# A new schedule for a decayed linear attention with a maxout layer behind it: items of 256 tokens, 64x64 tensor tiles, and an order planned at build time

## The chip, the cores and the metric

The kernel runs on one core of one Trainium2 chip. The metric is device time in microseconds, from the start of the program to its end; lower is better. The engines of the core work side by side and are named here as the profile names them: PE is TensorE (matrix multiply), PEld its loading of weights, DVE is VectorE, ACT is ScalarE, POOL is GpSimd, SP is SyncE, which here only issues transfers. A transfer (DMA) moves data between the chip's main memory and the core's on-chip memory; matrix products land in PSUM, which has eight banks.

## The reference

Inputs are q, k, v and alpha of 4 sequences, 8 heads, 768 tokens and 48 features, and three weight matrices. A state of 48 x 48 for each head decays by alpha and takes in k times v at every token; its product with q is the attention output. The heads are then joined to 384 features per token (3072 tokens in all), and a maxout layer follows.

```python
for t in range(S):
    state = alpha[:, :, t, :, None] * state + np.einsum('bhd,bhe->bhde', k[:, :, t], v[:, :, t])
    y[:, :, t] = np.einsum('bhd,bhde->bhe', q[:, :, t], state)
...
x = attn_out.transpose(0, 2, 1, 3).reshape(B * S, H * D)     # 3072 x 384
h1 = x @ w1                                                  # w1, w2: 384 x 1024
h2 = x @ w2
out = np.maximum(h1, h2) @ w_out                             # w_out: 1024 x 384
```

Everything is given and returned in float32.

## The kernel before

The recurrence is computed in chunks of 128 tokens, 24 of them ("items"). The logarithm of alpha is summed along the chunk by a matmul (`cs`); its exponentials scale q and k (`qt`, `kt`), both are turned by PE, scores are `kt` times `qt` under a triangular mask (`pt`), and `y` is the masked scores times v plus q times the carried state (`T16`). The state itself goes on through `kv` and `w`.

```python
def load(n):                        # four transfers of 192 KB, rows of 48 floats (192 bytes)
    b, c = divmod(n, NCH)
    for src, tag in ((alpha, "af"), (q, "qf"), (k, "kf"), (v, "vf")):
        t = ldp.tile([128, H, D], FP32, tag=tag, name=tag)
        nc.sync.dma_start(out=t, in_=src[b, :, c * C : (c + 1) * C, :].rearrange("h p d -> p h d"))
...
def p1(n):                          # PE: sums of the logarithm
    nc.tensor.matmul(cs[:, 0 : H * D], lhsT=cmat, rhs=loga[:, :, 0:D], start=True, stop=True)
    for r in range(NP):             # four small ones, whole-chunk sums
        nc.tensor.matmul(cs[0:112, o : o + 2], lhsT=lp[:, r, 0:112], rhs=gcol, start=True, stop=True)
def a2(n):                          # ACT: en, ep, gg (exponentials, written to SBUF)
    nc.scalar.activation(out=en, in_=csv, func=ACTF.Exp, scale=-1.0)
    nc.scalar.activation(out=ep, in_=csv, func=ACTF.Exp)
...
def v1(n):                          # qt on DVE, kt on POOL, v to 16 bit on POOL
    nc.vector.tensor_mul(out=qts[n % 2][:, :, 0:D], in0=qf, in1=s["ep"])
    nc.gpsimd.tensor_mul(out=kts[n % 2][:, :, 0:D], in0=kf, in1=s["en"])
...
def p2(n):                          # PE: eight transposes of 128 columns; v2 copies them to SBUF (qk)
    for r in range(NP):
        nc.tensor.transpose(tp[:, r, :], qp[:, r, :], ident16)
    for r in range(NP):
        nc.tensor.transpose(tp[:, NP + r, :], kp[:, r, :], ident16)
...
def p3(n):                          # PE: scores (two row tiles) and kv (two column tiles)
    for r in range(NP):
        for o, ps in ((0, pa), (64, pb)):
            nc.tensor.matmul(ps[:, r, :], lhsT=qk[o : o + D, NP + r, :], rhs=qk[o : o + D, r, :], ...)
...
def p4(n):                          # PE: y in blocks of 32 features, four column tiles
    for i in range(3):
        if not first:
            for r in range(NP):
                nc.tensor.matmul(y[32 * r : 32 * r + 32, i, :], lhsT=T16[0:112, r, i, :], rhs=s["qk"][0:112, r, :], ...)
        for t in range(2):
            for r in range(NP):
                nc.tensor.matmul(y[32 * r : 32 * r + 32, i, :], lhsT=v16[:, r, i, 16 * t : 16 * t + 32],
                                 rhs=s["pt"][:, t, r, :], ...)
```

The maxout layer uses max(h1, h2) = h2 + relu(h1 - h2). So only `h` = x (w1 - w2) goes through relu, and the part with h2 is x times m, where m = w2 w_out is computed once on the chip (`prep_t`, `prep_m`). `h` is made for groups of mostly 384 tokens, `op` for each 128.

```python
def fstep(a, W, f):                 # h for one of 8 blocks of 128 features, W tokens; relu on ACT or DVE
    for s in range(3):
        nc.tensor.matmul(h[:, 0:W], lhsT=wd16[:, s, f * 128 : (f + 1) * 128], rhs=xT[:, s, a : a + W], ...)
def tstep(a, i, half):              # out for 128 tokens: 3 matmuls with m, 8 with w_out; ACT evicts, SP stores
    ...
```

The order is written by hand: in each round the loads five items ahead, parts of three items' attention, and in between the gaps are filled from a list of dense steps (`gap`).

```python
for n in range(1, NCG + 1):
    if n - 1 + LD < NCG:
        load(n - 1 + LD)
    v1(n + 1)
    if n > 1:
        p4(n - 1)
        a3(n - 1)
    gap(1.05)
    ...
```

PSUM is split into three pools of three, two and three banks. Item 0 is loaded first, then w2, w1 and w_out as one transfer each, then items 1 to 4.

Of the kernel before, what the change touches and what calls it, by code (L numbers as in the profile page):

```python
# [9 lines left out]
FP16 = mybir.dt.float16  # L10
FP32 = mybir.dt.float32
ACTF = mybir.ActivationFunctionType
ALU = mybir.AluOpType


@with_exitstack
def kernel(
# [15 lines left out]

    nc = tc.nc
    B, H, S, D = q.shape
    C = 128
    NCH = S // C
    NCG = B * NCH  # L40
    NP = H // 2
    NT, DM = out.shape
    DFF = moe_w1.shape[1]
    NF = DFF // 128
    WMAX = 384

    ctx.enter_context(tc.manual_schedule())
    constp = ctx.enter_context(tc.tile_pool(name="constp", bufs=1))
    ldp = ctx.enter_context(tc.tile_pool(name="ldp", bufs=6))
    wk = ctx.enter_context(tc.tile_pool(name="wk", bufs=2))  # L50
    mo = ctx.enter_context(tc.tile_pool(name="mo", bufs=2))
    psx = ctx.enter_context(tc.tile_pool(name="psx", bufs=3, space=bass.MemoryType.PSUM))
    psp = ctx.enter_context(tc.tile_pool(name="psp", bufs=2, space=bass.MemoryType.PSUM))
    psm = ctx.enter_context(tc.tile_pool(name="psm", bufs=3, space=bass.MemoryType.PSUM))

    LD = 5
    nc.scalar.preload_act_table_set("natural_log_exp_and_others")

    loads = {}

    def load(n):
        b, c = divmod(n, NCH)
        got = []
        for src, tag in ((alpha, "af"), (q, "qf"), (k, "kf"), (v, "vf")):
            t = ldp.tile([128, H, D], FP32, tag=tag, name=tag)
            nc.sync.dma_start(  # L66
                out=t, in_=src[b, :, c * C : (c + 1) * C, :].rearrange("h p d -> p h d")
            )
            got.append(t)
        loads[n] = got  # L70


    w1f = constp.tile([128, 3, DFF], FP32)
    w2f = constp.tile([128, 3, DFF], FP32)
    wof = constp.tile([128, NF, DM], FP32)
# [6 lines left out]
    load(0)  # L82
    nc.sync.dma_start(out=w2f, in_=moe_w2.rearrange("(p s) f -> p s f", s=3))
    nc.sync.dma_start(out=w1f, in_=moe_w1.rearrange("(p s) f -> p s f", s=3))
    nc.sync.dma_start(out=wof, in_=moe_w_out.rearrange("(s p) d -> p s d", p=128))
    for n in range(1, LD):
        load(n)

    ident16 = constp.tile([128, 128], FP16)
    make_identity(nc, ident16)  # L90
    u16 = constp.tile([128, 128], FP16)
    make_upper_triangular(nc, u16, val=1.0, diag=True)
    half1 = constp.tile([128, 128], FP16)
    nc.gpsimd.memset(half1, 0.0)
    nc.gpsimd.memset(half1[0:64, :], 1.0)
    cmat = constp.tile([128, 128], FP16)
    nc.vector.tensor_sub(out=cmat, in0=u16, in1=half1)
    gcol = constp.tile([128, 2], FP16)
    nc.gpsimd.memset(gcol, 0.0)
    nc.gpsimd.memset(gcol[0:64, 0:1], 1.0)  # L100
    nc.gpsimd.memset(gcol[64:128, 1:2], 1.0)

    NB = 3
    logas = [constp.tile([128, H, 64], FP16, name=f"loga{i}") for i in range(2)]
    qts = [constp.tile([128, H, 64], FP16, name=f"qt{i}") for i in range(2)]
    kts = [constp.tile([128, H, 64], FP16, name=f"kt{i}") for i in range(2)]

    v16s = [constp.tile([128, NP, 3, 48], FP16, name=f"v16_{i}") for i in range(NB)]
    T16s = [constp.tile([128, NP, 3, 32], FP16, name=f"T16_{i}") for i in range(NB)]
    for i in range(2):  # L110
        for t in (logas, qts, kts):
            nc.vector.memset(t[i], 0.0)
    for t in v16s + T16s:
        nc.gpsimd.memset(t, 0.0)

    xT = constp.tile([128, 3, NT], FP16)


    st = {}

    def a1(n):
        if n < NCG:
            nc.scalar.activation(out=logas[n % 2][:, :, 0:D], in_=loads[n][0], func=ACTF.Ln)  # L123

    def p1(n):
        if n >= NCG:
            return
        loga = logas[n % 2]
        cs = psx.tile([128, H * D + 2 * NP], FP32, tag="x", name="cs")
        nc.tensor.matmul(cs[:, 0 : H * D], lhsT=cmat, rhs=loga[:, :, 0:D], start=True, stop=True)  # L130
        lp = loga.rearrange("p (r t) d -> p r (t d)", t=2)
        for r in range(NP):
            o = H * D + 2 * r
            nc.tensor.matmul(cs[0:112, o : o + 2], lhsT=lp[:, r, 0:112], rhs=gcol, start=True, stop=True)  # L134
        st[n] = {"cs": cs}

    def a2(n):
        if n >= NCG:
            return
        cs = st[n]["cs"]  # L140
        csv = cs[:, 0 : H * D].rearrange("p (h d) -> p h d", h=H)
        ep = wk.tile([128, H, D], FP32, tag="ep")
        en = wk.tile([128, H, D], FP32, tag="en")
        gg = wk.tile([128, NP, 2], FP32, tag="gg", bufs=4)
        nc.scalar.activation(out=en, in_=csv, func=ACTF.Exp, scale=-1.0)  # L145
        nc.scalar.activation(out=ep, in_=csv, func=ACTF.Exp)  # L146
        nc.scalar.activation(
            out=gg[0:112], in_=cs[0:112, H * D :].rearrange("p (r t) -> p r t", t=2), func=ACTF.Exp
        )
        st[n].update(ep=ep, en=en, gg=gg)  # L150

    def v1(n):
        if n >= NCG:
            return
        _, qf, kf, vf = loads[n]
        s = st[n]
        nc.vector.tensor_mul(out=qts[n % 2][:, :, 0:D], in0=qf, in1=s["ep"])  # L157
        nc.gpsimd.tensor_mul(out=kts[n % 2][:, :, 0:D], in0=kf, in1=s["en"])  # L158
        v16 = v16s[n % NB]
        vp = vf.rearrange("p (r t) (e s) -> p t r s e", t=2, s=3)  # L160
        for t in range(2):
            nc.gpsimd.tensor_copy(out=v16[:, :, :, 32 * t : 32 * t + 16], in_=vp[:, t])  # L162

    def vt(n):

        if n >= NCG or n % NCH == 0:
            return
        s = st[n]
        g = wk.tile([128, NP], FP32, tag="g")
        nc.gpsimd.tensor_mul(out=g[0:112], in0=st[n - 1]["gg"][0:112, :, 1], in1=s["gg"][0:112, :, 0])  # L170
        gb = g[0:112].unsqueeze(2).to_broadcast([112, NP, D])
        gs = gb.rearrange("p r (s e) -> p r s e", s=3)
        w = st[n - 1]["w"]
        ws = w.rearrange("p r (s e) -> p r s e", s=3)
        T16 = T16s[n % NB]
        nc.gpsimd.tensor_mul(out=T16[0:48, :, :, 0:16], in0=ws[0:48], in1=gs[0:48])  # L176
        nc.gpsimd.tensor_mul(out=T16[64:112, :, :, 16:32], in0=ws[64:112], in1=gs[64:112])
        if n % NCH < NCH - 1:
            t32 = wk.tile([128, NP, D], FP32, tag="t32")
            nc.gpsimd.tensor_mul(out=t32[0:112], in0=w[0:112], in1=gb)  # L180
            s["t32"] = t32

    def p2(n):
        if n >= NCG:
            return
        tp = psx.tile([128, 2 * NP, 128], FP16, tag="x", name="tp")
        qp = qts[n % 2].rearrange("p (r t) d -> p r (t d)", t=2)
        kp = kts[n % 2].rearrange("p (r t) d -> p r (t d)", t=2)
        for r in range(NP):
            nc.tensor.transpose(tp[:, r, :], qp[:, r, :], ident16)  # L190
        for r in range(NP):
            nc.tensor.transpose(tp[:, NP + r, :], kp[:, r, :], ident16)  # L192
        st[n]["tp"] = tp

    def v2(n):
        if n >= NCG:
            return
        qk = wk.tile([128, 2 * NP, 128], FP16, tag="qk", bufs=3)
        nc.vector.tensor_copy(out=qk, in_=st[n]["tp"])  # L199
        st[n]["qk"] = qk  # L200

    def p3(n):
        qk = st[n]["qk"]
        pa = psp.tile([128, NP, 128], FP32, tag="p", name="pa")
        pb = psp.tile([128, NP, 128], FP32, tag="p", name="pb")
        for r in range(NP):
            for o, ps in ((0, pa), (64, pb)):
                nc.tensor.matmul(  # L208
                    ps[:, r, :], lhsT=qk[o : o + D, NP + r, :], rhs=qk[o : o + D, r, :], start=True, stop=True
                )  # L210
        st[n]["pp"] = (pa, pb)
        if n % NCH < NCH - 1:
            kv = psx.tile([128, NP, D], FP32, tag="x", name="kv")
            kt, v16 = kts[n % 2], v16s[n % NB]
            for r in range(NP):
                for t in range(2):
                    nc.tensor.matmul(  # L217
                        kv[64 * t : 64 * t + 64, r, :],
                        lhsT=kt[:, 2 * r + t, :],
                        rhs=v16[:, r, :, 32 * t : 32 * t + 16],  # L220
                        start=True,
                        stop=True,
                    )
            st[n]["kv"] = kv

    def v3(n):
        s = st[n]
        pt = wk.tile([128, 2, NP, 128], FP16, tag="pt")
        ub = u16.unsqueeze(1).to_broadcast([128, NP, 128])
        for t in range(2):  # L230
            nc.vector.tensor_mul(out=pt[:, t], in0=s["pp"][t], in1=ub)  # L231
        s["pt"] = pt
# [31 lines left out]
    def a3(n):  # L264
        nc.scalar.copy(out=xT[:, :, n * C : (n + 1) * C], in_=st[n]["y"])  # L265
        if n > 1:
            del st[n - 2]
# [175 lines left out]
```

## Time and profile before

The time is 163.45 us, the median of 3 runs (162.66 to 165.11). The profile is of one execution, with a span of 161.4 us.

| | busy us | share of span |
|---|---|---|
| PE | 139.1 | 86% |
| PEld | 95.2 | 59% |
| DVE | 92.9 | 58% |
| ACT | 81.3 | 50% |
| POOL | 91.5 | 57% |

Matmuls are pipelined, so an engine that is shown busy is not always at its peak; the distance between the starts of two matmuls is the better measure. Some groups of instructions, with the mean time of one: `kt` 128x384 on POOL, 1015 ns; `qt` 128x384 on DVE, 1016 ns; `qk` 128x1024 on DVE, 691 ns; each half of `pt` about 680 ns; an exponential of 128x384 on ACT about 488 ns; relu of 128x384 on ACT 500 ns; the eviction of `out` 479 ns. All transfers together moved 28.65 MB, and nearly all of their 104648 packets were under 512 bytes. In a waits view each line reads: who waited for whom, us in all, how often, the longest.

### The profile page before, as it was taken

The page shows a single profiled execution, that of the slowest core. Times are in us where ns is not written, and L with a number is a line of the kernel's source. Part 1 is how long each engine was busy: PE and PEld are TensorE (multiplying, and loading weights), DVE is VectorE, ACT ScalarE, POOL GpSimd, SP SyncE. Part 2 cuts the span into 40 slices and gives each one's busy share as a digit, 9 for nine tenths or more (in the row PEclk, how much of TensorE's full clock was granted, in tenths as well). Part 3 has the DMA queues.
Part 4 walks back from the last instruction along what each step waited for, and adds up shares of the span by engine and source line. Part 5 has one row for each costly group of instructions (what it writes and reads, how often), then busy time and mean ns, then how long its engine had stood idle before and what let it go on. Part 6 is the DMA issues. An engine that isn't in the chain of part 4 may idle for free.

```text
span 161.4 us, 5077 instructions
## 1 busy us (share of the span) xinstructions
PE 139.1 (86%) x2056; PEld 95.2 (59%) x2056; DVE 92.9 (58%) x153; ACT 81.3 (50%) x216; POOL 91.5 (57%) x170
## 2 busy tenths in 40 slices
PE   0427169799996999999999999999999999999990
PEld 0316157467664667666766667666676667657660
DVE  4163962095668747866576766875587656841110
ACT  3302063564754574487338753775466557435341
POOL 7714555079867666777447767765376876700000
PEclk9999999999999599999999999999999999999999
DMA  5999999999989899989999979998989611012021
GB/s 106 278 411 389 275 201 162 195 188 173 199 158 235 176 201 160 225 175 231 204 224 180 222 154 236 196 230 177 216 168 220 129 55 49 0 53 97 17 84 51
DMA packets 104648, 28.65 MB, mean 178 GB/s; under 512 B 100272, under 2 KB 104368, under 8 KB 104368
## 3 DMA queue, kind: packets, MB, share of 16 engines
q1 hardware_dynamic: 104624, 28.32, 84.0%
q8 instruction: 16, 0.26, 0.7%
q14 instruction: 8, 0.07, 0.1%
HBM read 23.59 MB, written 4.72 MB: 175 GB/s over the span
## 4 chain that ended last, share of the span: by engine, by line
PE 78%; DMA 9%; ACT 3%; SPq 2%; issue 2%; DVE 2%; POOL 1%; ACTq 0%; DVEq 0%; POOLq 0%
PE h L308 22%; PE op L325 20%; DMA wof<-in_moe_w_out_dram 9%; PE op L322 8%; PE y L258 5%; PE pa L208 4%; PE y L252 3%; PE tp L192 3%; PE tp L190 3%; PE kv L217 3%; PE mp L296 2%; PE cs L130 2%; PE cs L134 2%; SPq L66 2%; DVE pt L231 1%
## 5 line engine op out<-in xcount | busy, mean ns | idle before, releaser
L157 DVE TENSOR_TENSOR qt<-qf,ep 128x384 f16<-128x384 f32 x24 | 24.4, 1016 | 34.4 <-ACT ep L146 34.4
L308 PE MATMUL h<-xT,wd 128*128 128x384 f16 (+2 forms) x264 | 40.2, 295 | 1.0 <-ACT g L313 0.6
L325 PE MATMUL op<-wo,g 128*128 128x384 f16 x192 | 38.5, 327 | 0.0
L158 POOL TENSOR_TENSOR kt<-kf,en 128x384 f16<-128x384 f32 x24 | 24.4, 1015 | 24.6 <-ACT en L145 21.1
L313 ACT ACTIVATE g<-h 128x384 f16<-128x384 f32 (+2 forms) x66 | 25.2, 410 | 10.7 <-PE h L308 10.4
L308 PEld LDWEIGHTS <-wd 128*128 128x128 f16 x264 | 22.0, 103 | 10.6 <-issue 2.6
L329 ACT COPY outs<-op 128x384 f32<-128x384 f32 x24 | 11.5, 479 | 30.9 <-PE op L325 30.9
L162 POOL CAST v<-vf 128x192 f16<-128x192 f32 x48 | 26.9, 587 | 0.0
L325 PEld LDWEIGHTS <-g 128*128 128x128 f16 x192 | 17.4, 98 | 11.1
L199 DVE COPY qk<-tp 128x1024 f16<-128x1024 f16 x24 | 16.6, 691 | 9.8 <-PE tp L192 9.0
L145 ACT ACTIVATE en<-cs 128x384 f32<-128x384 f32 x24 | 11.7, 489 | 15.7 <-PE cs L134 14.0
L176 POOL TENSOR_TENSOR T<-w,g 48x192 f16<-48x192 f32 x20 | 10.0, 501 | 14.4 <-DVE w L239 11.9
L231 DVE TENSOR_TENSOR pt<-pa,u 128x512 f16<-128x512 f32 x24 | 16.4, 685 | 2.9 <-PE pb L208 2.9
L130 PE MATMUL cs<-loga,cmat 128*128 128x384 f16 x24 | 8.1, 338 | 10.0 <-ACT loga L123 10.0
L231 DVE TENSOR_TENSOR pt<-pb,u 128x512 f16<-128x512 f32 x24 | 16.3, 678 | 0.0
L258 PE MATMUL y<-pt,v 128*32 128x128 f16 x576 | 15.7, 226 | 0.0
L322 PE MATMUL op<-m,xT 128*128 128x384 f16 x72 | 15.7, 327 | 0.0
L311 DVE TENSOR_SCALAR g<-h 128x384 f16<-128x384 f32 (+2 forms) x22 | 9.7, 440 | 10.3 <-PE h L308 10.3
L134 PEld LDWEIGHTS <-loga 128*112 128x112 f16 x96 | 9.1, 137 | 9.8 <-issue 7.8
L123 ACT ACTIVATE loga<-af 128x384 f16<-128x384 f32 x24 | 12.9, 539 | 1.8 <-DMA af<-in_alpha_dram 1.8
L265 ACT CAST xT<-y 128x384 f16<-128x384 f32 x24 | 11.8, 490 | 3.9 <-PE y L258 3.9
L258 PEld LDWEIGHTS <-v 128*32 128x32 f16 x576 | 11.8, 100 | 0.5 <-issue 0.4
(55 smaller groups left out, 185.5 us busy)
## 6 DMA issues: line engine op xcount, KB each, us to landing
af<-in_alpha_dram SPq DMA_DIRECT2D x24, 192.0 KB, 4.1
qf<-in_q_dram SPq DMA_DIRECT2D x24, 192.0 KB, 4.5
kf<-in_k_dram SPq DMA_DIRECT2D x24, 192.0 KB, 4.7
vf<-in_v_dram SPq DMA_DIRECT2D x24, 192.0 KB, 4.4
out_dram<-outs SPq DMA_DIRECT2D x24, 192.0 KB, 3.2
w2f<-in_moe_w_dram SPq DMA_DIRECT2D x1, 1536.0 KB, 8.1
w1f<-in_moe_w_dram SPq DMA_DIRECT2D x1, 1536.0 KB, 10.9
wof<-in_moe_w_out_dram SPq DMA_DIRECT2D x1, 1536.0 KB, 14.7
```

The source lines that it names most:

```text
L123: nc.scalar.activation(out=logas[n % 2][:, :, 0:D], in_=loads[n][0], func=ACTF.Ln)
L134: nc.tensor.matmul(cs[0:112, o : o + 2], lhsT=lp[:, r, 0:112], rhs=gcol, start=True, stop=True)
L157: nc.vector.tensor_mul(out=qts[n % 2][:, :, 0:D], in0=qf, in1=s["ep"])
L158: nc.gpsimd.tensor_mul(out=kts[n % 2][:, :, 0:D], in0=kf, in1=s["en"])
L162: nc.gpsimd.tensor_copy(out=v16[:, :, :, 32 * t : 32 * t + 16], in_=vp[:, t])
L199: nc.vector.tensor_copy(out=qk, in_=st[n]["tp"])
L231: nc.vector.tensor_mul(out=pt[:, t], in0=s["pp"][t], in1=ub)
L258: nc.tensor.matmul(y[32 * r : 32 * r + 32, i, :], lhsT=v16[:, r, i, 16 * t : 16 * t + 32], rhs=s["pt"][:, t, r, :], start=(first and t == ...
L308: nc.tensor.matmul(h[:, 0:W], lhsT=wd16[:, s, f * 128 : (f + 1) * 128], rhs=xT[:, s, a : a + W], start=(s == 0), stop=(s == 2))
L313: nc.scalar.activation(out=gts[a][:, f, 0:W], in_=h[:, 0:W], func=ACTF.Relu)
L322: nc.tensor.matmul(op, lhsT=xT[:, s, t0 : t0 + C], rhs=m16[:, s, :], start=(s == 0), stop=False)
L325: nc.tensor.matmul(op, lhsT=gts[a][:, f, i * C : (i + 1) * C], rhs=wo16[:, f, :], start=False, stop=(f == NF - 1))
```

## The change

The attention and the layer behind it compute the same thing; how they are cut and in which order they run is new.

- Items are 256 tokens, two to a partition (`j`): a load row holds two neighbouring tokens of a head, 384 bytes. Weights come in four pieces each, and all loads share 20 buffers.
- The sum of the logarithm is taken over token pairs first (`su`, DVE), then along the pairs by one matmul for each half of the heads; a second matmul takes the odd token out again. The chunk for the state is 128 tokens as before (64 pairs, `x` = 0 or 1).
- `ep` is written back into PSUM in place; `qt` reads it there.
- The transposes of items 0 to 4 stay on PE (`TURN`); for items 5 to 11 they are DMA transposes issued from SP, two of 256 KB for each item.
- `kv`, scores and the value part of `y` run on 64x64 tiles of PE; `y` comes in blocks of 64 features that straddle heads, by sliding windows into zero-padded `v16` and `T16`.
- PSUM is one tensor of eight banks; attention steps take a pair of banks, dense steps one.
- All steps are given to a planner with dependences, engines that may run them and their assumed durations, buffers and a priority. It runs through time once while the program is built, puts the step with the lowest priority number that is ready on each engine that is free, and the program is emitted in that order. Several evictions and casts may go to ACT or DVE, as the plan has it.

```diff
-    C = 128
+    NDB = S // 256
+    TURN = (0, 1, 2, 3, 4)
...
-            t = ldp.tile([128, H, D], FP32, tag=tag, name=tag)
-            nc.sync.dma_start(
-                out=t, in_=src[b, :, c * C : (c + 1) * C, :].rearrange("h p d -> p h d")
-            )
+            t = A["ld", n, which] = ldp.tile([128, H, 2 * D], FP32, tag="ld", name=which + "f")
+            nc.sync.dma_start(
+                out=t, in_=src[b, :, c * 256 : (c + 1) * 256, :].rearrange("h (p j) d -> p h (j d)", j=2)
+            )
...
+    seq = [("d", 0)] + [("w2", i) for i in range(4)] + [("w1", i) for i in range(4)] + [("wo", i) for i in range(4)]
+    seq += [("d", n) for n in range(1, ND)]
...
+            for g in range(2):
+                nc.tensor.matmul(t[:, g, 0:384], lhsT=cmat,
+                                 rhs=s16[:, 4 * g : 4 * g + 4, 0:D].unsqueeze(2).to_broadcast([128, 4, 2, D]), ...)
+                nc.tensor.matmul(t[:, g, 0:384].rearrange("p (h j d) -> p h j d", h=4, j=2)[:, :, 0, :], lhsT=nid16,
+                                 rhs=l1[:, 4 * g : 4 * g + 4, :], start=False, stop=True, skip_group_check=True)
...
+            t = A["cs", n][:, :, 0:384]
+            nc.scalar.activation(out=t, in_=t, func=ACTF.Exp)
...
+        if n in TURN:
+            ...                      # 16 PE transposes, two copies by DVE or ACT
+        else:
+            def e_tr(eng, a):
+                nc.sync.dma_start_transpose(out=new_qk()[:, a].rearrange("p j r m -> p (j r) m"),
+                                            in_=qkts[i3][:, a].rearrange("p j h d -> p (j h d)"))
...
+                                nc.tensor.matmul(      # scores: 32 per item
+                                    t[64 * x : 64 * x + 64, u, c0 : c0 + 128].rearrange("p (j m) -> p j m", j=2),
+                                    lhsT=qk[o : o + D, 1, j, r, 64 * x : 64 * x + 64],
+                                    rhs=qk[o : o + D, 0, :, r, 64 * x : 64 * x + 64], ...)
...
+            for i in range(12):                        # y: 48 value matmuls, four tiles in turn
+                for x, u in ((0, 0), (1, 1), (0, 1), (1, 0)):
+                    todo.append(lanes[x, u][i])
...
+    for g, nch in enumerate((2, 3, 3, 3, 3, 3, 3, 2, 2)):
+        group(g, c0, nch)                              # dense groups of 256 or 384 tokens
+        c0 += nch
+    for o in plan.run():
+        o.emit(o.eng)
```

The aim is less work on PE for attention, fewer and longer rows in the transfers, and an order without the gaps of one that is written by hand.

## The prediction

> **What bounds the kernel now.** I read the page from the top (busy time, slices), then the busy time by stretches, then TensorE's timeline inside one steady stretch, and last the waits, each to answer what the one before left open.
>
> The page's first two parts (busy us and share by engine; then the span in 40 slices of about 4 us):
> ```profile
> PE 139.1 (86%) x2056; PEld 95.2 (59%) x2056; DVE 92.9 (58%) x153; ACT 81.3 (50%) x216; POOL 91.5 (57%) x170
> ...
> PE   0427169799996999999999999999999999999990
> DMA  5999999999989899989999979998989611012021
> ```
> PE is full from the eighth slice on; before that it is mostly empty. The DMA row is full until two thirds of the span and then drops, so it is near its limit, but is it what PE waits for? The stretches answer (busy us and count of each engine, granted clock, DMA share):
> ```profile
> 0.00:20.00 20.00, 6.72 (x77) 4.98 (x78) 10.21 (x19) 4.49 (x8) 10.66 (x25) 1.00 0.95 294
> 20.00:32.00 12.00, 9.39 (x72) 6.92 (x72) 3.77 (x6) 6.18 (x17) 4.97 (x9) 1.00 1.09 184
> 61.00:140.00 79.00, 79.00 (x1228) 53.08 (x1226) 54.25 (x86) 45.75 (x120) 53.01 (x98) 1.00 0.89 175
> 157.60:161.40 3.80, 0.00 (x0) 0.00 (x0) 0.00 (x0) 0.43 (x1) 0.00 (x0) 1.00 0.15 54
> ```
> From 61 to 140 us PE never stops, DVE, ACT and POOL are at about two thirds, and DMA goes on beside it. The ends are the other cost: 20 us with a third of PE's time used, a half-used stretch after it, and 3.8 us at the end for the last eviction and store. Busy can hide pipelining, so I took PE's rates from starts in its timeline (start us, us, engine, line, tiles):
> ```profile
> 94.59 0.33 PE L130 MATMUL cs<-loga,cmat 128*128 128x384 f16 x1
> 94.76 0.32 PE L134 MATMUL cs<-gcol,loga 128*112 128x2 f16 x4
> 95.01 0.24 PE L252 MATMUL y<-qk,T 112*32 112x128 f16 x4
> ...
> 95.64 0.66 PE L322 MATMUL op<-m,xT 128*128 128x384 f16 x3
> 96.14 0.65 PE L325 MATMUL op<-wo,g 128*128 128x384 f16 x3
> 96.72 0.23 PE L208 MATMUL pa<-qk 48*128 48x128 f16 x1
> ...
> 96.90 0.22 PE L208 MATMUL pb<-qk 48*128 48x128 f16 x1
> 97.05 0.31 PE L217 MATMUL kv<-v,kt 128*64 128x48 f16 x8
> ```
> Start to start: op, 3 matmuls in 0.49 us, 163 ns each. cs with its four small sums 0.42 (94.59 to 95.01), y 0.63 (to 95.64), pa, pb and kv 0.57 (96.72 to the next group at 97.29) and about 0.09 to enter them; the eight transposes, elsewhere in the timeline, 0.44. That is 2.15 us of attention per 128 tokens. The dense layers take 24 matmuls per 384 tokens for h (8 x 0.163 = 1.30 per 128) and 11 for op (1.79). Sum 5.24. The h stretches of the chain of waits recur at 86.52, 102.13, 117.68 and 133.29 us: 15.6 us per three items, 5.20 each. So the steady part is TensorE's own throughput, with no gap left in it. In the waits, PE's only large one is at the start:
> ```profile
> DVE qt L157 <- ACT ep L146: 34.4, 22, 5.6
> POOL kt L158 <- ACT en L145: 21.1, 18, 5.1
> PE cs L130 <- ACT loga L123: 10.0, 3, 4.6
> ```
> The first two are engines with spare time, and cost nothing; the third is item 1's decay waiting behind the weights' DMA.
>
> **What the Trainium skill says.** "TensorEngine Tiling (Array Packing)", Key Properties: different tiles load weights and multiply in parallel, and changing the tiling mode drains the array. The trace agrees with both: pa and pb matmuls start in pairs every 56 to 60 ns, and from the last pb (96.90) to the first kv (97.05) it is 0.15, so a switch costs about 0.09 us. "SBUF — State Buffer", SBUF: two separate sides: the port pair of VectorE and GpSimd is an exclusive lock, and a VectorE operation with two SBUF inputs takes part in it. It fits: qt averages 1016 ns, but its first instance took 0.56 us where it began just ahead of kt. "DMA: Bandwidth & Descriptors", Specifications: rows under 512 B do not reach line rate; the trace's 192-byte rows go at one 192 KB load per about 1.0 us, near 196 GB/s, and the two weights that follow at 1536 KB per 4.2 us (landings at about 15.5 and 19.75 us), near 374. Same page, Latency and other measured facts: DMA transposes reach 261 GB/s; no run here shows one yet.
>
> **The change part by part.**
>
> *Loads.* From the two rates above, the bytes of 192 KB cost 4.2/8 = 0.53 us and 1024 rows cost the remaining 0.47. A new load is 384 KB in 1024 rows: 1.05 + 0.47 = 1.5 us (an estimate), so 6.1 per 256 tokens instead of 8.0. The weights in 12 pieces with 1 KB and 1.5 KB rows cost about 1.2 each, 14.5 instead of 12.6. Over the kernel about 23 us of DMA time fewer, less 14 transposes of 256 KB at about 1.0 (estimate from the skill's rate), 14 us. Except in the start DMA did not set the time, so this buys little directly.
>
> *TensorE, per 256 tokens.* Matmul times by the rates above: cs, 2 x 163 for 384 columns, 2 x about 83 for 192, 4 small at 52: 0.70. kv, 32 matmuls on four 64x64 tiles, eight rounds; the old kv's four column pairs take 0.24 less a switch, 0.037 a round: 0.30. Scores, 32 matmuls of 128 columns, eight rounds of 56 ns: 0.45. y, 16 state matmuls two abreast (8 x 0.056 = 0.45) and 48 value matmuls four abreast (12 x 0.056 = 0.67): 1.12. Mode switches, about eight at 0.095: 0.76. Sum 3.33. Old, without transposes, 2 x (2.15 - 0.44) = 3.42. So 64x64 tiles save only 0.09 per item: the 32-column tiles of the old y were already four abreast. With the transposes (16 x 0.056 = 0.90) the first five items are no cheaper than before (4.23 against 4.30); the seven whose transposes go to DMA save about 0.97.
>
> *Sum of PE.* New: dense layers 24 x 3.09 = 74.2, attention 12 x 3.33 = 40.0, transposes 5 x 0.90 = 4.5, less 1.3 for first and last items of a sequence = 117.4. Old: 24 x 5.24 less 1.7 = 124.1. Both have about 5.3 of weight preparation (mp 24 x 0.163 = 3.9, 24 weight transposes). So the change takes about 7 us out of the bound.
>
> *The start.* New order: item 0, w2, w1, w_out, then items 1, 2, ... With 6.1 for item 0 after some 2.2 of first latency and 14.5 for weights, w_out lands near 23 us. By then PE can have done item 0 (4.2), weight transposes (1.4) and the first h group of two chunks (2.6). Item 1 lands 24.5 to 29, item 2 30.5 to 35, item 3 near 41; from alpha's landing to xT I count about 11 us (Ln, cs, two Exp, kt on POOL near 2.0, copies, pt, y). Group 1 needs half of item 2, so its h starts near 43 us. Until then PE gets mp, the first outputs (3.6), items 1 and 2, and a piece of 3. Done by 43 us: about 25 us. In the old kernel 157.5 - 129.4 = 28 us of PE's time are lost in all, mostly before 32 us; here about 18 by 43 us. The order worked out at build time, which puts whatever is ready on PE, is what fills it.
>
> *Other engines.* ACT: Ln and Exp on 768 columns save a fixed part each; 12 x (0.83 + 0.81 + 0.81 + 0.18) = 32 instead of 41. DVE: qt reads exp from PSUM, so no second SBUF operand: from 24.4 to about 12 x 0.96 = 11.5, and seven of twelve qk copies vanish. POOL: kt 2.0, v cast 1.2, four T and two t32 at 0.5, g 0.2, 6.4 per item, 77 in all. ACT and DVE share relu and evictions. Each stays at or under two thirds of a 10 us item. Off the path.
>
> *End.* 25 us by 43; remaining 122.7 - 25 = 97.7 gives 140.7. I add 4 us, about 4% of that, for gaps from a fixed order that can't match every real duration and from eight PSUM banks shared by pairs and singles (my choice, not read off). Tail 3.9 as now: 148.6 of span. The measured median is 2 above the profile's span (163.45 and 161.4); I take half of that: 149.5.
>
> **Rivals.** (a) PSUM as the new bound. cs, kv, scores and y each take two of eight banks. With three pairs held, h has two banks, and one h (0.49 us) plus PE's latency and a relu of 0.50 comes to about 1.2 per bank, so 0.6 per h instead of 0.49. If that held for all 72 h steps (nine groups of eight) it would add some 8 us: 157. Against it: h is taken whenever a bank is free, and the old kernel ran full with three. (b) SyncE's one in-order queue. A transpose that waits for kt holds the loads and stores behind it, and a transpose behind queued loads lands late; PE's order is fixed, so each late one stalls it. At 1 us each, 14 of them make 14: 160, no gain. For it: loads already wait about 1 us each on SyncE now. Against: loads run up to five items ahead, and late items are backed by dense work. (c) The plan fills the start better than I think, by attention running far ahead, and gaps are near nil: 140. (d) False waits, since all PSUM is now one tensor: if bank reuse were tracked coarsely, PE would serialise with evictions, well above 165. I think waits go by bank.
>
> **Range and chances.** (a) to (c) give 140 to 160 around 149.5; I take 140 to 159 for 8 in 10. "Within 2%" is 160.2 to 166.7 and needs (b) in full or half of (d); "slower" needs (d) or a worse start. Chances: faster 0.87, within 2% 0.07, slower 0.06.
>
> **What would show it.** Right: PE full from about 43 us, dense groups still 163 ns a matmul, about 3.3 us of attention starts per item without transposes, first out stores near 28 us, qt near 0.48 us per half. Wrong: PE waits on DMA transposes or on relu in the middle; loads far from 1.5 us; 64x64 rounds longer than 56 ns, which would mean that four tiles are not abreast; a switch dearer than 0.1 us. A wrong start would show as PE still under half busy at 45 us.

## The result, and the profile after

The changed kernel takes 170.75 us (median of 4 runs, 170.19 to 173.56) against 163.12 us before: a ratio of 1.046, with a 95% interval from 1.041 to 1.051. It is slower; I had predicted 149.5 us and a range of 140 to 159. Its profiled execution has a span of 168.3 us.

The page of the changed kernel, first two parts (busy time; then the span in 40 slices of 4.2 us: TensorE, the clock granted to it, the transfers):

```profile
PE 134.8 (80%) x2144; PEld 89.6 (53%) x2144; DVE 77.8 (46%) x136; ACT 84.1 (50%) x155; POOL 71.5 (42%) x113
...
PE   0058599967884868969599894789989999999991
...
PEclk9999999999999699999879999699999999999999
DMA  5999999999999999999999999967210212103112
```

PE was 139.1 us busy before and is 134.8 us busy now, in a longer span. So the work on the bounding engine did shrink; the time lost beside it grew. The PE row is no longer a full block: it is full only in the last quarter, after the DMA row has emptied between 109 and 118 us. The clock row has three dips in the middle (each is a spell of 3.4 us at half clock); before, there was one:

```profile
PEclk9999999999999599999999999999999999999999
```

The same kernel by stretches (busy us and count of PE, PEld, DVE, ACT, POOL; then granted clock, DMA share, GB/s):

```profile
32.00:43.00 11.00, 8.65 (x205) 6.33 (x205) 6.83 (x13) 4.43 (x7) 8.64 (x15) 1.00 1.14 263
43.00:62.00 19.00, 14.11 (x404) 10.88 (x403) 14.77 (x25) 10.58 (x18) 13.68 (x20) 0.91 1.08 265
62.00:90.00 28.00, 23.01 (x363) 14.12 (x364) 15.27 (x27) 15.96 (x30) 14.44 (x23) 0.94 1.17 237
90.00:120.00 30.00, 25.91 (x572) 16.40 (x561) 16.92 (x28) 12.32 (x23) 16.92 (x26) 0.94 1.04 195
120.00:168.30 48.30, 43.80 (x393) 27.75 (x391) 4.60 (x7) 23.70 (x53) 0.00 (x0) 1.00 0.16 58
```

Before, PE was busy for all 79 us from 61 to 140. Now it stands idle for 4.9 of the 19 us from 43 to 62, 5.0 of 28, 4.1 of 30, and the half-clock spells take about 5 us more from these stretches (19 x 0.09 + 28 x 0.06 + 30 x 0.06). What it didn't do there it does at the end: from 120 us on it works for 43.8 us with POOL at rest and DMA nearly so.

To split the difference I added up the starts of all matmuls in both traces, and counted a distance between two starts that is above 0.4 us as idle (less 0.18 us for the matmul itself), and all else as work. Before: first matmul at 4.4 us, work 137.8, idle 14.9; together the last start at 157.1. After: 8.5, 132.1, 24.0; 164.5. So work is 5.8 us less, idle 9.0 us more, and the start 4.1 us later. The work includes the half clock and waits under 0.4 us.

The waits of the changed kernel (who waited for whom: us in all, times, longest):

```profile
ACT loga L418 <- DMA af<-in_alpha_dram: 18.8, 12, 3.4
POOL v L489 <- DMA vf<-in_v_dram: 12.8, 5, 8.1
...
PE PS L435 <- DVE s L425: 8.5, 1, 8.5
...
PE PS L620 <- DMA qk<-qkt: 5.1, 3, 3.1
```

Before, ACT waited once for alpha's load:

```profile
ACT loga L123 <- DMA af<-in_alpha_dram: 1.8, 1, 1.8
```

Now Ln waits for it at all twelve items, 18.8 us. ACT has time to spare (84.1 us busy), so its idle would seem to cost nothing. A piece of the timeline shows why it does cost (start us, us, engine, line):

```profile
79.91 0.82 PE L701 MATMUL PS<-xT,wd 128*128 128x384 f16 x4
...
81.44 0.84 ACT L418 ACTIVATE loga<-af 128x768 f16<-128x768 f32 x1 [2.30 <-DMA af<-in_alpha_dram]
...
82.19 0.57 ACT L338 CAST xT<-PS 128x384 f16<-128x384 f32 x1
...
82.62 0.49 ACT L711 ACTIVATE g<-PS 128x384 f16<-128x384 f32 x1
82.81 0.77 PE L701 MATMUL PS<-xT,wd 128*128 128x384 f16 x2 [2.07 <-ACT xT L338]
```

ACT reached item 9's Ln and stood 2.30 us until alpha landed. Behind the Ln in ACT's fixed order were the copy of a finished y into xT (L338), which PE's next h matmuls (L701) read, and a relu (L711). PE ran out at 80.7 and stood 2.07 us. The wait is put down to ACT; its origin is the transfer two steps back.

### The profile page after: what moved, and what is told of

Same layout as the page of the kernel before. It is cut to its first block, busy times and chain, and to the rows that moved or that the text cites. A ratio compares the mean times of both kernels' runs of the same rounds, so it can differ in the third digit from the quotient of the medians.

```text
span 168.3 us, 5032 instructions
## 1 busy us (share of the span) xinstructions
PE 134.8 (80%) x2144; PEld 89.6 (53%) x2144; DVE 77.8 (46%) x136; ACT 84.1 (50%) x155; POOL 71.5 (42%) x113
## 4 chain that ended last, share of the span: by engine, by line
PE 49%; DMA 26%; DVE 7%; POOL 5%; SPq 4%; issue 4%; ACT 3%; DVEq 0%; ACTq 0%; POOLq 0%
PE PS L701 13%; PE PS L728 13%; DMA af<-in_alpha_dram 11%; DMA qk<-qkt 8%; PE PS L674 6%; PE PS L726 5%; DMA vf<-in_v_dram 4%; DMA w2f<-in_moe_w_dram 3%; PE PS L392 3%; SPq L295 3%; DVE pt L628 2%; PE PS L620 2%; POOL qkt L474 2%; PE PS L435 2%; PE PS L510 1%
## 5 line engine op out<-in xcount | busy, mean ns | idle before, releaser
L701 PE MATMUL PS<-xT,wd 128*128 128x384 f16 (+1 forms) x216 | 37.6, 319 | 3.9 <-ACT xT L338 2.6
L728 PE MATMUL PS<-wo,g 128*128 128x384 f16 x192 | 37.2, 326 | 0.0
L628 DVE TENSOR_TENSOR pt<-PS,mask 128x1024 f16<-128x1024 f32 x24 | 28.1, 1217 | 3.8 <-PE PS L620 3.5
L701 PEld LDWEIGHTS <-wd 128*128 128x128 f16 x216 | 20.3, 99 | 15.8 <-issue 4.7
L474 POOL TENSOR_TENSOR qkt<-kf,en 128x768 f16<-128x768 f32 x12 | 21.7, 1813 | 14.9 <-ACT gg L460 6.9
L711 ACT ACTIVATE g<-PS 128x384 f16<-128x384 f32 (+1 forms) x55 | 24.5, 458 | 6.3 <-PE PS L701 5.9
L338 ACT COPY outs<-PS 128x384 f32<-128x384 f32 x23 | 11.0, 478 | 28.2 <-PE PS L728 28.2
L418 ACT ACTIVATE loga<-af 128x768 f16<-128x768 f32 x12 | 10.1, 843 | 18.8 <-DMA af<-in_alpha_dram 18.8
L726 PE MATMUL PS<-m,xT 128*128 128x384 f16 x72 | 15.7, 326 | 0.0
L575 POOL TENSOR_TENSOR T<-w,gg 48x192 f16<-48x192 f32 x24 | 12.9, 539 | 4.3 <-DVE w L600 3.4
L480 DVE TENSOR_TENSOR qkt<-qf,PS 128x384 f16<-128x384 f32 x24 | 12.0, 546 | 4.0 <-DMA qk<-qkt 4.0
L674 PE MATMUL PS<-pt,v 64*64 64x128 f16 x576 | 12.0, 233 | 0.1
L338 ACT CAST xT<-PS 128x384 f16<-128x384 f32 x13 | 7.6, 585 | 7.5 <-PE PS L701 4.5
L340 DVE CAST xT<-PS 128x384 f16<-128x384 f32 x11 | 6.5, 588 | 10.2 <-PE PS L701 5.4
```

Source lines behind the costliest of these rows:

```text
L338: nc.scalar.copy(out=out, in_=in_)
L474: e.tensor_mul(out=hjd(qkts[i3], 1), in0=A["ld", n, "k"].rearrange("p h (j d) -> p h j d", j=2), in1=A["en", n].rearrange("p g (h j d) -> ...
L480: nc.vector.tensor_mul(out=hjd(qkts[i3], 0)[:, 4 * g : 4 * g + 4], in0=A["ld", n, "q"].rearrange("p h (j d) -> p h j d", j=2)[:, 4 * g : 4 ...
L575: e.tensor_mul(out=T16s[m % 4][o : o + 48, :, 48 * u : 48 * u + 48], in0=w_[o : o + 48], in1=g_[o : o + 48])
L628: nc.vector.tensor_mul(out=t.rearrange("p u r c -> p (u r) c"), in0=A["sc", n, hf].rearrange("p u (r c) -> p (u r) c", r=2), in1=mask.rear ...
L674: nc.tensor.matmul(dst, lhsT=lhsT, rhs=rhs, start=(x, u) not in begun, stop=ends[x, u] == i, skip_group_check=True)
```

## The experiments

All ratios are to the kernel before, measured on the same chip. For reference: the changed kernel is at 170.75 us.

**e1: the DMA transposes left out, the order kept.** Items 5 to 11 score with the turned q and k of items 2 to 4, so the output differs.

```diff
     for o in plan.run():
+        if o.name[:2] in ("dk", "dq"):
+            n = int(o.name[2:])
+            A["qk", n] = A["qk", 2 + (n - 5) % 3]
+            continue
         o.emit(o.eng)
```

> The order of all instructions is kept; only the 14 DMA transposes are left out, and items 5 to 11 score with the turned q and k of items 2 to 4 (so the output is not the reference's). Theory DMA (the transposes take the transfer queue's time, loads and stores behind them come late, and every engine's fixed order stalls on it): 14 x 1.9 = 27 us of transfer time go, loads move ahead, and most of the 20 us of TensorE idle after 43 us goes with it: span 150 to 158. Theory order (the plan's durations are too short everywhere, and a fixed order loses at each step): only the direct waits on transposes go, about 5 us: span 162 to 166.

Measured 163.06 us (ratio 0.998, 0.995 to 1.001), span 161.1. That is 7.7 us back, between the two theories and nearer to that of the order: more than the direct waits of 5.1 us on transposes, less than all idle. In its profile idle by the starts of matmuls falls from 24.0 to 15.5 us, while the half-clock spells grow from 10.2 to 17.0 us.

**e2 and e5: the loads of items 5 to 11 left out, and then loads and transposes.** The items read the tiles of items 1 to 4 again, so the output differs; the order is kept.

```diff
+        if o.name[:3] in ("lda", "ldq", "ldk", "ldv") and int(o.name[3:]) >= 5:
+            n = int(o.name[3:])
+            A["ld", n, o.name[2]] = A["ld", 1 + (n - 5) % 4, o.name[2]]
+            continue
```

> The order is kept; the 28 loads of items 5 to 11 are left out, and these items read the tiles of items 1 to 4 again (so the output is not the reference's). The 14 transposes stay. Theory DMA: 28 x 1.37 = 38 us of transfer time go, transposes land promptly, span 150 to 156. Theory transposes alone (their own latency and their issue on SyncE stall the scores): the waits of scores on transposes stay, span 160 to 166. Theory order: 160 to 165.

> The order of the changed kernel is kept; both the 14 DMA transposes and the 28 loads of items 5 to 11 are left out (these items read tiles of items 1 to 4, so the output is not the reference's). After about 45 us no transfer but stores is left. If late transfers are behind the TensorE idle after 43 us (leaving out either one gave 7 to 12 us back), the two gains add up in part: span 151 to 156. If each run already gave back all that transfers cost, and what remains is computed steps that the fixed order waits for, it is that of the run without loads, 156 to 159.

Without the loads two runs took 157.62 and 160.12 us (spans 155.7 and 157.2, at the edge of what the theory DMA said); without both 159.90 (2 runs; ratio 0.980, 0.974 to 0.986). The two gains do not add: with the later loads gone, the transposes cost nothing more. The page of the run without both:

```profile
PE   0057689994998489999899999899889999999991
...
PEclk9999999998699955999999999999999999999999
DMA  5999999999991000002100111002100402122202
```

The transfers end at about 50 us, and the later part of PE's row is nearly full. What remains is before 62 us: the start, and two dips of the clock. So on the given order late transfers cost about 11 to 13 us, and some 10 us above my prediction have another source.

**e3: all twelve items turned by TensorE**, `TURN = tuple(range(12))`, planned anew.

> All twelve items are turned by TensorE, and the order is planned anew for it; the result is the reference's. It costs TensorE 7 x 0.9 = 6.3 us and takes 27 us off the transfers. Theory DMA: time 158 to 164. Theory order: the slip of some 20 us against the plan stays and TensorE's 6.3 us are added, 172 to 177.

Measured 174.34 us (ratio 1.068, 1.058 to 1.078). The theory that transposes take the queue's time and that this sets the end fails here: 27 us of transfers are gone, and the kernel is slower by 2 to 4 us (its four runs go from 172.47 to 175.62). The queue's row (packets, MB, time that the packets took as a share of 16 engines' span), of the changed kernel, of e3 and of the kernel before, also measures a transpose:

```profile
q1 hardware_dynamic: 72448, 31.99, 81.7%
```

```profile
q1 hardware_dynamic: 57664, 28.32, 64.5%
```

```profile
q1 hardware_dynamic: 104624, 28.32, 84.0%
```

0.817 x 168.3 = 137.5 us and 0.645 x 170.7 = 110.1 us; the difference over 14 transposes is 1.96 us each. Before the change the queue took 0.840 x 161.4 = 135.6 us. So the longer rows saved 25.5 us of packet time and the transposes spent 27.4: nothing was saved. Packet times overlap, so this is not the time for which a transfer holds up the next: the DMA share of a stretch goes up to 1.17, and a 384 KB load has 1.7 us of packet time although loads land 1.3 to 1.5 us apart.

**e4 and e9: the same operations, planned with longer durations taken from the trace.** e4 changes transfers and engines in the plan, e9 the transfers alone. Only the order of emission differs from the changed kernel. The edit of e9:

```diff
-                    o.seen = dma + 0.6
+                    o.seen = dma + 1.9
...
-    LX = 1024 * 20.5 / 16e3            # 1.31, one load
+    LX = 1.37
...
-    WX = 384 * 1024 / 400e3            # 0.98, one piece of a weight
+    WX = 1.25
...
-            ck = plan.add(f"dk{n}", {"SP": 1.2}, ..., xfer=1.15)      # and the same for dq
+            ck = plan.add(f"dk{n}", {"SP": 1.2}, ..., xfer=1.9)
```

The 1.25 for a weight piece and the 1.9 for a transpose are packet times; the pieces landed 1.1 us apart. So these figures are on the safe side and not exact. e4 also sets pt to 1.22, xT to 0.58 (ACT) and 0.59 (DVE), qt to 1.1, su to 0.4, the v cast to 0.83 and each setup part on DVE to 6.0.

> The same operations with the same transposes by DMA, planned with the durations that the trace shows (load 1.37, weight piece 1.25, transpose 1.9, landing 1.9 after the transfer, pt 1.22, xT 0.58, setup on DVE 6.0). Theory order: the engines' orders fit what happens and 8 to 12 us come back, 158 to 163. Theory DMA: the queue is full to about 115 us whatever the order, and little comes back: 166 to 172.

> The changed kernel planned with measured durations for transfers alone (load 1.37, weight piece 1.25, transpose 1.9, landing 1.9 after the transfer); the durations of the engines stay as they were. If late transfers that the plan didn't foresee are what the fixed order loses by (Ln on ACT placed ahead of ready evictions), this alone gives what the full new plan gave: 162.5 to 165.5. If the engines' durations matter as much: 166 to 169.

Measured: e4 163.94 us (ratio 1.005, 1.002 to 1.007), e9 160.68 us (0.985, 0.975 to 0.995); e4 is just outside its 158 to 163, and e9 better than its 162.5 to 165.5. The numbers for transfers in the plan give 10 us back, with every transfer still there; as much, within 1 to 3 us, as leaving the transfers out under the old order. The half-clock spells take 10.2 us in e9 as in the changed kernel; idle by the starts falls from 24.0 to 16.6 us. This is the theory that stands: not the amount of transfers, but an order that expects them earlier than they come. The same two lines of the waits in e9:

```profile
POOL v L489 <- DMA vf<-in_v_dram: 14.7, 5, 8.5
...
ACT loga L418 <- DMA af<-in_alpha_dram: 9.9, 5, 3.0
```

Ln waits 9.9 us at five items instead of 18.8 at twelve. In e1 and e2 this wait is 10.8 and 7.0 us. But no run moves Ln alone, so its share of the 10 us is not known. e4 gains 3.3 us less than e9. About 1 us of that can be the engines' durations: so much lies between e8 and e13 below, which differ in them without the 6.0 for the setup. The 6.0 moves item 0's first matmul from 8.5 to 15.3 us in the trace; that this is the rest is my guess.

**e6: two PSUM banks kept for dense steps.** Attention may take three of the four pairs.

```diff
-        for i in range(0, 8, 2):
+        for i in range(0, 6, 2):
             if self.banks[i] and self.banks[i + 1]:
```

> The changed kernel with its own durations, but attention may take only the first three pairs of PSUM banks; two banks are always left for the dense steps. Theory PSUM (attention holds all four pairs while DVE works off the masks, and the ready dense steps find no bank from 44 to 58 us): the idle and the half-clock spell between 43 and 62 us go, time 165 to 168. Theory order and DMA: the same waits come elsewhere, 169 to 173.

Measured 168.51 us (1.034, 1.028 to 1.039): about 2 us, just outside what the PSUM theory said. h of group 1 starts at 54.9 instead of 58.5 us, but the clock between 43 and 62 us was no better in its profile (0.84).

**e7: dense groups (2, 2, 2, 3, 3, 3, 3, 3, 3)** instead of (2, 3, 3, ..., 2, 2), so that the second waits for item 1 alone.

> The changed kernel with its own durations; dense groups of 2, 2, 2 and then 3 chunks instead of 2, 3, 3, ... so that the second group needs item 1 alone and not item 2. If TensorE lacked ready dense work between 31 and 58 us because a group waited for item 2, h of group 1 starts near 42 us instead of 58.5, and time is 166 to 169. If transfers and the fixed order set the end, the idle moves later and the time stays at 169 to 172.

Measured 171.05 us (1.050, 1.044 to 1.056): nothing. h of group 1 does start at 48.0 instead of 58.5 us, and PE idles 3.0 instead of 4.9 us between 43 and 62; but between 62 and 120 it idles 12.0 instead of 9.1 us. The gain is lost again later, while transfers still come late; which wait takes it was not tried.

**e8 and what is in it.** e8 puts together e4's durations without the 6.0 for the setup, e7's groups, e6's banks, item 1 loaded ahead of the weights, and the negative identity written by ACT.

```diff
-    seq = [("d", 0)] + [("w2", i) for i in range(4)] + ...
-    seq += [("d", n) for n in range(1, ND)]
+    seq = [("d", 0), ("d", 1)] + [("w2", i) for i in range(4)] + ...
+    seq += [("d", n) for n in range(2, ND)]
...
-        nc.vector.tensor_scalar_mul(out=nid16, in0=ident16, scalar1=-1.0)
+        nc.scalar.activation(out=nid16, in_=ident16, func=ACTF.Copy, scale=-1.0)
```

> A version that is meant to beat both: planned with the measured durations, groups 2, 2, 2, 3, ..., item 1 loaded before the weights, two banks kept for dense steps, and the negative identity written by ACT so that no VectorE step waits for GpSimd's memsets at the start. If the four causes add: 155 to 160. If the fixed order's slip after the transfers stays at 5 us and nothing else comes back: 161 to 164.

Measured 155.86 us (0.954, 0.947 to 0.960): faster than both kernels. Then parts were taken out again. e10 has the old durations in the plan, e11 the old load order, e12 all transposes on TensorE, e13 the old durations for the engines but the measured ones for transfers, e14 the old groups and all four bank pairs.

> The best version so far (155.9) with the old durations in the plan; load order, groups, kept banks and the start stay. Theory order: its gain is mostly that the plan fits the transfers, and 6 to 10 us are lost: 162 to 166. If the earlier second item is what counts: 156 to 159.

> The best version with the old load order (item 1 after all weights). If TensorE's lack of ready work before 43 us and its half-clock spells come from item 1's late data: 159 to 162. If the plan's durations are what counts: 155.5 to 158.

> The best version with all transposes on TensorE, planned anew. It costs TensorE 7 x 0.9 = 6.3 us and takes 27 us off a transfer queue that is full to about 128 us. If the DMA transposes pay in a plan that knows their cost: 160 to 163. If they cost as much in waits as they save: 155 to 158.

> The best version with measured durations for transfers alone and the old ones for the engines. If the plan's transfers are the cause: 154 to 157.5, like the best version. If the engines' durations are part of the 9 us that the old durations cost: 159 to 163.

> The best version with the old dense groups (2, 3, 3, ...) and with all four bank pairs open to attention. If dense work that is ready early and finds a bank matters once transfers are planned right: 158 to 161. If these two are worth as little as on the changed kernel: 155.5 to 158.

| run | us | ratio to before (95% interval) |
|---|---|---|
| e8, all together | 155.86 | 0.954 (0.947 to 0.960) |
| e10, old durations in the plan | 164.63 | 1.007 (1.004 to 1.010) |
| e11, item 1 loaded after the weights | 157.83 | 0.970 (0.963 to 0.976) |
| e12, all transposes on TensorE | 161.09 | 0.989 (0.985 to 0.992) |
| e13, measured durations for transfers alone | 154.66 | 0.951 (0.946 to 0.956) |
| e14, old groups and banks | 158.17 | 0.967 (0.960 to 0.974) |

The durations are worth 8.8 us, the load order 2.0, groups and banks together 2.3; e13 shows that of the durations only those of the transfers count. The runs of e8 alone spread over 2 us (154.40 to 156.42), so the two smaller figures are rough. e10 and e13 differ only in the plan's numbers for transfers, as the changed kernel and e9 do: 10 us each time, on two sets of groups, banks and load order. A change of the engines' numbers alone, which moves the order too, gains nothing (e13 to e8). With the transfers' numbers right, the DMA transposes pay: e12 loses 5.2 us, near the 6.3 us of TensorE work that they take away. In e10 the direct waits of scores on transposes are back at 6.0 us and Ln's wait at 15.5 us:

```profile
POOL v L489 <- DMA vf<-in_v_dram: 19.3, 6, 5.4
ACT loga L418 <- DMA af<-in_alpha_dram: 15.5, 9, 3.7
...
PE PS L620 <- DMA qk<-qkt: 6.0, 6, 2.1
```

The best version, e13, by its page and its stretches:

```profile
PE 128.2 (83%) x2144; PEld 85.3 (55%) x2144; DVE 78.8 (51%) x136; ACT 82.1 (53%) x153; POOL 73.7 (48%) x115
...
PE   0036797599999689996799999997988999999990
...
PEclk9999999999999999999999999999999999999999
DMA  4999999999999999999999999899999411102122
...
q1 hardware_dynamic: 72448, 31.99, 93.3%
```

```profile
43.00:62.00 19.00, 17.13 (x394) 12.57 (x391) 15.48 (x30) 12.03 (x25) 12.40 (x18) 1.00 1.17 277
62.00:90.00 28.00, 25.75 (x500) 16.70 (x493) 18.15 (x29) 14.49 (x30) 17.31 (x27) 1.00 1.20 225
90.00:120.00 30.00, 27.95 (x469) 17.09 (x468) 14.79 (x25) 17.47 (x34) 14.10 (x20) 1.00 1.20 228
120.00:153.70 33.70, 29.47 (x349) 17.76 (x345) 6.24 (x7) 14.31 (x30) 1.02 (x2) 1.00 0.20 64
```

The transfers are the same as in the changed kernel, now 93.3% of a shorter span and full to about 119 us, and PE is nearly full beside it, at full clock. At 120 us 29.5 us of PE's work are left instead of 43.8. So a full transfer queue was not the bound by itself.

## Why the prediction was wrong

**The bound and the work per item: right; the sum of PE's work: short.** I put PE's work at 7 us less than before; the starts show 5.8 us less with the half clock, which I had left out, in it. The parts hold: cs 0.60 us in the trace (0.70 predicted), kv 0.37 (0.30 and a switch), scores 0.68 (0.45 and switches), y 1.36 (1.12 and switches). Four 64x64 tiles are abreast, and they save next to nothing, as said. But the sum from which I counted, 129.4 us before and 122.7 after, stands against 137.8 and 132.1 by the starts. Of the 28 us that I took as lost in the old kernel, only 19 were by this count (14.9 of idle and the 4.4 before the first matmul).

**The engines off the path: right in kind.** From the page of the changed kernel:

```profile
L628 DVE TENSOR_TENSOR pt<-PS,mask 128x1024 f16<-128x1024 f32 x24 | 28.1, 1217 | 3.8 <-PE PS L620 3.5
...
L474 POOL TENSOR_TENSOR qkt<-kf,en 128x768 f16<-128x768 f32 x12 | 21.7, 1813 | 14.9 <-ACT gg L460 6.9
...
L620 PE MATMUL PS<-qk 48*64 48x128 f16 x384 | 9.5, 233 | 9.6 <-DMA qk<-qkt 5.1
...
L480 DVE TENSOR_TENSOR qkt<-qf,PS 128x384 f16<-128x384 f32 x24 | 12.0, 546 | 4.0 <-DMA qk<-qkt 4.0
```

qt fell to 546 ns a half (0.48 predicted), kt is 1.81 us (2.0), pt 1.22 us. None became a bound.

**Transfers: half right.** Loads landed 1.3 to 1.5 us apart (1.5 predicted). A transpose took 1.96 us of packet time, twice the 1.0 that I worked out from the Trainium skill's 261 GB/s ("DMA: Bandwidth & Descriptors", Latency and other measured facts). That is a figure of this loaded queue: the same difference is 1.68 us a transpose between e2 and e5 and 2.43 between e8 and e12. From the start of its first packet to the end of its last, a transpose of the changed kernel took 0.93 to 2.98 us. So the skill's rate was reached at the best (256 KB in 0.93 us are 282 GB/s), but not on average. Of the 9 us of transfer time that I had saved (7, with the 1.9 us that the pieces of the weights add), none was. I had also read the transfers' row before as full to two thirds of the span; it was full to 125 of 161 us.

**The start: half right.** I said that about 18 us of PE's time would be lost by 43 us; PE was busy for 28.0 of the 43 (26.6 before the change), so 15 were lost. That this came out near was luck, since it was done with other work: the first h group came at 28.2 us, not before 23, the first store was issued at 39.5 and not near 28, and group 1's h started at 58.5 instead of 43.

**The step that failed is the term "4 us for gaps from a fixed order" after 43 us.** It measured about 15 us of idle between 43 us and the end, not counting the last store. Beside it, PE was busy for 106.8 us in that time where my sum had 97.7; 5 of these 9 us are half clock. I had chosen the 4 and not read it off, and I had the right mechanism in hand as rival (b), but too narrowly: I looked at transposes that stall the scores (5.1 us in the waits) and counted late loads as harmless because they run ahead. e2 shows that without later loads 11 to 13 us come back, e9 that a plan which knows when they land gets 10 us with all of them. Rival (a), PSUM, is real but worth about 2 us (e6). Rival (c), gaps near nil, is refuted by the 15 us. Rival (d), false waits that put the time well above 165, is refuted by e13, which has the same single PSUM tensor.

**What stays open.** e13 is at 154.7, still 5 us above what I had predicted for the change; PE's work by the starts is 126.9 us in it, 4 above my sum. Which of the transfers' numbers counts most was not tried. How the half-clock spells begin was not tried either: e8, e12 and e13 have none before their last 2 us, but e1 has more of them than the changed kernel with less idle.

## What to carry to other kernels

In a program whose order is fixed at build time, an engine with spare time is not harmless: what it waits for can be paid by everything behind it in its queue. Before planning or trusting such an order, measure when transfers land in the full kernel, with the queue loaded, and not alone; here a 1.3 us error in the landing, 0.27 us in a weight piece and 0.75 us in a transpose, together, cost 10 us. When a big rewrite moves the time the wrong way, run its operations in another order before dropping any of them.

## What the runs showed of the hardware

A transpose by DMA of 128 x 1024 16-bit elements, in packets of 256 bytes, adds 1.68 us (e2 less e5, with few loads beside it), 1.96 us (changed kernel less e3) or 2.43 us (e8 less e12) to the packet time of the queue, over 16 engines. It lands 4.3 us after its issue (median, changed kernel), a load of alpha 6.1:

```profile
af<-in_alpha_dram SPq DMA_DIRECT2D x12, 384.0 KB, 6.1
...
qk<-qkt SPq DMA_TRANSPOSE x14, 4.3
```

GpSimd memsets hold up VectorE at the start. The timeline of the changed kernel:

```profile
3.12 2.10 POOL L262 MEMSET v<- 128x768 f16 x3
...
3.35 3.78 DVE L256 TENSOR_SCALAR nid<-ident 128x128 f16<-128x128 f16 x1
...
5.15 1.93 POOL L276 MEMSET T<- 128x512 f16 x4
...
8.05 0.36 DVE L425 TENSOR_TENSOR s<-loga 128x384 f16<-128x384 f16 x1
```

A 128x128 scaling with an immediate took 3.78 us, from 3.35 to 7.13, while GpSimd wrote zeros in seven instructions (3.12 to 7.08); it got no turn between them and ended when they did. This fits the Trainium skill ("SBUF — State Buffer", SBUF: two separate sides): the ports that VectorE and GpSimd share are an exclusive lock, and the one that starts first has it for its whole instruction. The skill says this for some VectorE operations only; that this scaling is one of them, no run shows by itself. Here GpSimd only writes. Moving that one operation to ACT (e8) left the first matmul where it was, at 8.4 us, since the mask copies behind it are still on VectorE.
